# Holding each of the first 40 loads of a fused attention and gated-MLP kernel until the load four places in front of it has landed

## Chip, core and metric

The kernel runs on one core of a Trainium2 chip. The metric is the device time of one execution in microseconds (us), as a median of several runs. Engines are named as in the profile: PE (TensorE, matmuls), PEld (its weight loads), DVE (VectorE), ACT (ScalarE), POOL (GpSimd) and SP (SyncE, which here only waits and issues DMAs; its rows carry the name SPq).

## What is computed

Chunked attention, then an RMS norm and a gated MLP, all in float32:

```python
for c in range(S // 32):                       # q, k, v: (4, 8, 768, 64)
    k_ctx = k[:, :, max(0, 32*c - 16):min(S, 32*c + 40)]
    k_full = np.concatenate([mem_k, k_ctx], axis=2)      # 8 memory keys in front
    v_full = ...                                         # the same of v
    a = softmax(q_c @ k_full.T / 8)
    out[:, :, 32*c:32*c + 32] = a @ v_full
x = out.transpose(0, 2, 1, 3).reshape(3072, 512)
xn = x / sqrt(mean(x*x) + 1e-6) * rms_g
g = xn @ w_gate                                # 512 x 1536
y = (silu(g) * (xn @ w_val)) @ w_out           # w_out: 1536 x 512
```

## The kernel before

**Tiling.** Attention is cut into 32 units: batch, half of the sequence (384 tokens), pair of heads. A unit u needs three loads from DRAM, all laid out beforehand so that each is one plain transfer to 128 partitions: q (192 KB), k (312 KB) and v (384 KB). Four units with the same batch and half make one block of 384 tokens for the MLP, so there are eight blocks. The MLP's weights are cut into twelve slices of 128 hidden columns, loaded in eight groups of one or two slices for each of the three matrices (512 KB or 1,024 KB a load). Each weight and each activation is split into a high and a low part, and a product is made of three matmul passes.

**Stages.** The first stage does the attention of blocks 0 and 1 (units 0 to 7), loads and splits the weights between it, and runs the MLP of these blocks as soon as weights are there. It follows a list written out by hand, ORDER: a token is a step, with `U`n for the loads of q and k of unit n (`load_qk`), `V`n for its v (`load_v`), `Z` for the next load of weights (`w_load`), `S`n for its scores (tile s, L204), `M`, `a`, `E`, `d`, `n` for the softmax, `P`n for the transposes (pT, L283), `O`n for the product with v (o, L300), `B` and `D` for the split of the result, `G` for the sums of squares (ss, L635), `J`, `F`, `f`, `I`, `H`, `L` for turning a load of weights into its high and low part, and `g`, `v`, `o` for the MLP's products (pg, pv, po). In this stage every engine keeps the written order. Afterwards come blocks 2 and 3 with the remaining units' attention spread between their products, and then blocks 4 to 7, whose weights come back from DRAM in prepared parts.

**The queue.** Every load of q, k, v and weights is issued by SP with `nc.sync.dma_start`, in the order of the list. SP is one queue: an issue that waits holds up all issues behind it. In this text the loads are numbered by their place on SP, from 1: q0, k0, q1, k1, q2, k2, the first gate weights, q3, k3, q4, k4, q5, k5, v0, the first value weights, v1 (16), q6, k6, v2, the first output weights (20), v3, v5, v4, q7, k7, v7 (26), the second gate group (27, the first of 1,024 KB), the second value group (28), v6 (29), and from 30 to 40 weights alone.

**Waits that stand there already.** A landing is told by one of eight semaphores (DMAHW0 to DMAHW7), used in turn. A load may only be issued when the load that used its semaphore before has landed, which is the one eight places in front; so at most eight loads are under way. One tiny load from the ACT queue (rms_g) has the first use of DMAHW0. Besides, a load waits until its buffer is free: six buffers each for q, k and v (`u % 6`), and three staging buffers for weights.

Of the kernel before, what the change touches and what calls it, by code (L numbers as in the profile page):

```python
# [69 lines left out]
SEQ = ([(0, f) for f in range(FA)] + [(1, f) for f in range(FA)] + [(b, f) for f in range(FA, FC) for b in range(2)]  # L70
       + [(1, f) for f in range(FC, FF // P)])


ORDER = """
U0 U1 U2 Z U3 S0 U4 M0 a0 U5 S1 M1 a1 V0 S2 E1 E0 M2 d0 J Z V1 U6 S3 a2 n0 E2 M3 P0 V2 F S4 Z C0a a3 m0a n1 E3
# [15 lines left out]
def tile_kernel(ctx: ExitStack, tc: tile.TileContext, q, k, v, w_gate, w_val, w_out, rms_g, out):  # L91
    nc = tc.nc
# [52 lines left out]
    def late_buffers(i):  # L145
# [5 lines left out]
        else:  # L151
# [2 lines left out]
            t = p1.tile([P, KN + VN + HT], F32, name="kv0", tag="ws")  # L154
            late["kv", 0], late["pt", 1] = t[:, 0:KN + VN], t[:, KN + VN:]

    def load_qk(u):
        d = st.setdefault(u, {})
        if u < NE:
            d["q"] = early.tile([P, HT], F32, name=f"q{u}", tag=f"q{u % 6}")  # L160
            t = early.tile([P, KN], F32, name=f"k{u}", tag=f"k{u % 6}")
            nc.sync.dma_start(out=d["q"], in_=q[u])
        else:

            t = late["kv", u % 2][:, 0:KN]
            d["q"] = late["q", u % 2]
            nc.sync.dma_start(out=d["q"], in_=q[u])
        d["k"] = t.rearrange("p (j k) -> p j k", j=NJ)
        nc.sync.dma_start(out=t, in_=k[u])

    def load_v(u):
        t = early.tile([P, VN], F32, name=f"vw{u}", tag=f"v{u % 6}") if u < NE else late["kv", u % 2][:, KN:]
        st.setdefault(u, {})["v"] = t.rearrange("p (j h d) -> p j h d", j=NJ, h=2)
        nc.sync.dma_start(out=t, in_=v[u])

    def pt_of(u):

# [204 lines left out]
    def w_load():  # L382
        c = wpos["load"]
        if c >= len(wchunks):
            return
        wpos["load"] += 1
        w, k = wchunks[c]
        f, n = WGROUPS[k]
        d = wst[c] = {}
        j = c - wfirst[1]  # L390
        if j < 0:
            pool = stage if c % 3 else p1
            tag = str(c % 3) if c % 3 else ""
            s = pool.tile([P, 2, DM, 2], U32, name=f"ws{c}", tag="ws" + tag)[:, 0:n]
        elif j % 3 == 2:
            s = p1.tile([P, 1, DM, 2], U32, name=f"ws{c}", tag="wy")
        else:
            if j % 3 == 0:
                wst["pair"] = p1.tile([P, 2, DM, 2], U32, name=f"ws{c}", tag="ws")
            s = wst["pair"][:, j % 3:j % 3 + 1]  # L400
        d.update(n=n, low=s[:, :, :, 0], high=s[:, :, :, 1], top=s.bitcast(F16)[:, :, :, 1])
        nc.sync.dma_start(out=s.rearrange("p n f t -> p n (f t)"),
                          in_={"g": w_gate, "v": w_val, "o": w_out}[w][f:f + n].bitcast(U32).rearrange("n p f -> p n f"))

    def w_open(c):
# [100 lines left out]
    def moe_t(g, vv, blk):  # L506
        g = silu_r(g, blk)
        t = silu_a(g)
        silu_b(t, g)
        moe_m(t, vv)  # L510
        return t
# [51 lines left out]
    def late_steps():  # L563
# [3 lines left out]
        for n in range(len(pairs) + 1):  # L567
# [27 lines left out]
            for u in new:  # L595
                load_qk(u)
# [15 lines left out]
            for u in cur if n else ():  # L612
                load_v(u)
# [4 lines left out]
    def tok_R(n):  # L618
        late_buffers(0)
        load_qk(NE)  # L620
        load_v(NE)
# [74 lines left out]
    def tok_o(n):  # L696
# [5 lines left out]
    steps = dict(  # L702

        U=load_qk, V=load_v, Z=lambda n: w_load(), W=warm, R=tok_R,

        S=stage_s, M=stage_ma, a=stage_mb, E=stage_e, d=lambda k: stage_da(2 * k), n=stage_db,
# [511 lines left out]
    for blk, fs in segments:  # L1218
# [10 lines left out]
        for n, f in enumerate(fs):  # L1229
# [28 lines left out]
            elif blk < 3:  # L1258
                with tc.high_priority():
                    t = moe_t(g, vv, blk)  # L1260
                xs = split_x(late_x["x"], t, out_, lambda h: moe_out(fs[-1], h, po, **edge))
            else:
                with tc.high_priority():
                    t = moe_t(g, vv, blk)
# [91 lines left out]
```

## Time and profile before

| what | us |
|---|---|
| median of 3 runs | 668.07 |
| lowest and highest of them | 666.81, 669.07 |
| the profiled execution | 671.41 |
| its span, first to last instruction | 669.6 |

The rows further down come from the profiled execution alone. In a timeline a row gives the start, the duration, the engine, the line, the operation and the tiles (written <- read), with a count when alike instructions follow each other; in square brackets stands the idle time in front of it and what ended it. A row of a DMA issue gives the tiles, the count, the size in KB and the time from the start of the issue to the landing; so start plus that time is the moment of landing. A row of the view by stretches gives the stretch, its length, the busy time of the five engines with their counts, then the granted share of PE's clock (1.00 is 2.4 GHz, 0.50 is 1.2 GHz), the share of time in which the DMA engines were busy, and GB/s. That last share can pass 1 a little, since packets on one engine overlap.

### The profile page before, as it was taken

The numbers are of one execution on the slowest core, as the hardware profiler recorded it, in microseconds if no ns is written. First come the engines' busy times: TensorE is split into PE (matmuls) and PEld (weight loads), VectorE is DVE, ScalarE is ACT, GpSimd is POOL, SyncE is SP. The second block draws the span as 40 slices with busy tenths as digits, with TensorE's granted clock in tenths as the row PEclk, the third lists the DMA queues.
The fourth block names the chain that finished last, engine by engine and source line by source line (L and its number), as shares of the span: only waits on it lengthen the run. The fifth ranks groups of instructions, "written<-read, shape, count | busy, mean of one in ns | idle before, by whom it ended". The sixth has DMA issues, their size and how long they took to land.

```text
span 669.6 us, 15527 instructions
## 1 busy us (share of the span) xinstructions
PE 657.9 (98%) x6238; PEld 612.1 (91%) x6238; DVE 503.3 (75%) x1020; ACT 334.7 (50%) x642; POOL 4.7 (1%) x12
## 2 busy tenths in 40 slices
PE   6999999999999999999999999999999999999998
PEld 4898999999899999989999999999888899999997
DVE  6699999777688788877859567569638378888964
ACT  4779887843434435354445454345335233434553
POOL 0010000000000000000000000000000000000000
PEclk8699999999999999999999999999999999999999
DMA  9645454249698778345439779797643599987102
GB/s 324 251 159 181 185 189 146 106 135 351 187 374 302 254 247 291 107 168 165 143 126 369 262 235 308 253 294 256 191 142 116 170 352 331 320 303 265 52 9 71
DMA packets 82039, 145.46 MB, mean 217 GB/s; under 512 B 7472, under 2 KB 34608, under 8 KB 81968
## 3 DMA queue, kind: packets, MB, share of 16 engines
q1 hardware_dynamic: 80096, 141.32, 62.2%
q10 hardware_dynamic: 1872, 3.15, 1.4%
q8 instruction: 49, 0.80, 0.5%
q14 instruction: 22, 0.18, 0.1%
HBM read 109.84 MB, written 34.60 MB: 216 GB/s over the span
## 4 chain that ended last, share of the span: by engine, by line
PE 88%; DVE 4%; DMA 3%; ACT 2%; issue 1%; SPq 0%; DVEq 0%
PE pg L473 14%; PE po L523 14%; PE pv L473 13%; PE po L1195 8%; PE mva L949 7%; PE mga L949 7%; PE pa L1115 4%; PE mve L949 3%; PE mge L949 3%; PE pe L1115 2%; PE s L220 2%; PE oe L314 2%; PE mgc L949 2%; PE mvc L949 2%; PE pT L283 1%; DMA kv<-qp 1%
## 5 line engine op out<-in xcount | busy, mean ns | idle before, releaser
L473 PE MATMUL pg<-xh,wh_g 128*128 128x384 f32 x192 | 67.3, 351 | 0.7 <-DVE rg L482 0.7
L473 PE MATMUL pg<-xh,wl_g 128*128 128x384 f32 x192 | 65.3, 340 | 0.0
L473 PE MATMUL pg<-xl,wh_g 128*128 128x384 f32 x192 | 65.2, 340 | 0.0
L473 PE MATMUL pv<-xh,wh_v 128*128 128x384 f32 x192 | 65.2, 339 | 0.0
L473 PE MATMUL pv<-xl,wh_v 128*128 128x384 f32 x192 | 64.9, 338 | 0.0
L473 PE MATMUL pv<-xh,wl_v 128*128 128x384 f32 x192 | 64.8, 338 | 0.0
L949 PE MATMUL mva<-x,r 128*128 128x384 f32 x288 | 58.2, 337 | 0.1
L949 PE MATMUL mga<-x,r 128*128 128x384 f32 x288 | 58.2, 337 | 0.1
L523 PE MATMUL po<-wh_o,hh 128*128 128x512 f32 x141 | 56.7, 402 | 0.0
L523 PE MATMUL po<-wl_o,hh 128*128 128x512 f32 x141 | 55.7, 395 | 0.0
L523 PE MATMUL po<-wh_o,hl 128*128 128x512 f32 x141 | 55.7, 395 | 0.0
L949 PEld LDWEIGHTS mga<-x,r 128*128 128x128 f32 x288 | 50.5, 188 | 0.8 <-ACT spare L921 0.4
L949 PEld LDWEIGHTS mva<-x,r 128*128 128x128 f32 x288 | 50.6, 188 | 0.5 <-DVE h L932 0.4
L182 ACT CAST hh<-t 128x384 fp32r<-128x384 f32 x45 | 23.2, 515 | 49.4 <-PE po L523 32.9
L1195 PE MATMUL po<-r,hhs 128*128 128x512 f32 x144 | 45.5, 397 | 0.0
L473 PEld LDWEIGHTS pg<-xh,wh_g 128*128 128x128 f32 x192 | 36.4, 189 | 3.3 <-DVE rg L482 1.0
L473 PEld LDWEIGHTS pg<-xl,wh_g 128*128 128x128 f32 x192 | 36.5, 190 | 1.3
L473 PEld LDWEIGHTS pv<-xh,wh_v 128*128 128x128 f32 x192 | 36.0, 188 | 0.4
L473 PEld LDWEIGHTS pg<-xh,wl_g 128*128 128x128 f32 x192 | 36.3, 189 | 0.0
L473 PEld LDWEIGHTS pv<-xl,wh_v 128*128 128x128 f32 x192 | 36.1, 188 | 0.3
L473 PEld LDWEIGHTS pv<-xh,wl_v 128*128 128x128 f32 x192 | 36.0, 188 | 0.0
L494 DVE TENSOR_TENSOR t<-t,pv 128x384 f32<-128x384 f32 x48 | 26.4, 550 | 10.7 <-PE pv L473 9.5
(252 smaller groups left out, 1600.2 us busy)
## 6 DMA issues: line engine op xcount, KB each, us to landing
r<-kg SPq DMA_DIRECT2D x84, 256.0 KB, 4.9
r<-kv SPq DMA_DIRECT2D x84, 256.0 KB, 4.4
r<-ko SPq DMA_DIRECT2D x68, 256.0 KB, 3.9
kv<-in_v_dram SPq DMA_DIRECT2D x24, 384.0 KB, 4.8
kv<-in_k_dram SPq DMA_DIRECT2D x24, 312.0 KB, 4.1
ws<-in_moe_w_gate_dram SPq DMA_DIRECT2D x4, 1024.0 KB, 4.8
ws<-in_moe_w_val_dram SPq DMA_DIRECT2D x4, 1024.0 KB, 4.8
ws<-in_moe_w_out_dram SPq DMA_DIRECT2D x4, 1024.0 KB, 4.9
```

Of the source, the lines that this page charges most:

```text
L182: return nc.scalar.copy(out, in_)
L220: on_pe(nc.tensor.matmul(d["s"][a:a + CH, o:o + KC], lhsT=d["q"][r, c * CH:c * CH + CH], rhs=d["k"][r, c // 2, 40 * cp:40 * cp + KC], star ...
L283: on_pe(nc.tensor.transpose(out=t[:, i * P:(i + 1) * P], in_=pe[:, i * P:(i + 1) * P], identity=ident))
L314: on_pe(nc.tensor.matmul(o2[cp][64 * hh:64 * hh + 64, o:o + CH], lhsT=st[u]["v"][r, j, hh], rhs=pt[r, j, hh ^ u % 2], start=True, stop=True))
L473: on_pe(nc.tensor.matmul(ps[:, 0:HT], lhsT=weight(a, n, f, kt), rhs=xs[c][:, kt], start=kt == 0 and i == 0, stop=kt == NKT - 1 and i == 2))
L494: nc.vector.tensor_tensor(out=t, in0=t, in1=vv, op=ALU.mult)
L523: on_pe(nc.tensor.matmul(po[i], lhsT=h[a][:, i * P:(i + 1) * P], rhs=weight(c, "o", f), start=f == first and n == 0, stop=f == end and n = ...
L949: on_pe(nc.tensor.matmul(bank[w, b], lhsT=r[:, a, kt], rhs=x[:, c, kt], start=bool(first) and kt == 0 and i == 0, stop=kt == 1 and i == 2, ...
L1115: on_pe(nc.tensor.matmul(bank[c][i], lhsT=uhl[u][x][:, i * P:(i + 1) * P], rhs=w[y], start=p == 0 and n == 0 and m in (1, 2, 5), stop=p == ...
L1195: on_pe(nc.tensor.matmul(po[i], lhsT=cur[a][:, i * P:(i + 1) * P], rhs=r[c], start=f == n == 0, stop=f == NF - 1 and n == 2))
```

## The change

A new helper `held` issues the load and keeps a list of what it has sent. From the fifth load on, and up to the fortieth, it adds a dependency on the load four places in front; this is a wait on that load's semaphore in front of the issue. `load_qk`, `load_v` and `w_load` call it in place of `nc.sync.dma_start`.

```diff
+HELD = 4
+    sent = []
+
+    def held(**kw):
+        i = nc.sync.dma_start(**kw)
+        i = getattr(i, "ins", i)
+        if HELD <= len(sent) < 40:
+            tc.add_manual_dep(i, sent[-HELD].name, mybir.DependencyInfo(mybir.DependencyClass.Sync, mybir.DependencyReason.DATA),
+                              reason="few loads in flight")
+        sent.append(i)
...
-            nc.sync.dma_start(out=d["q"], in_=q[u])
+            held(out=d["q"], in_=q[u])
...
-        nc.sync.dma_start(out=t, in_=k[u])
+        held(out=t, in_=k[u])
...
-        nc.sync.dma_start(out=t, in_=v[u])
+        held(out=t, in_=v[u])
...
-        nc.sync.dma_start(out=s.rearrange("p n f t -> p n (f t)"),
+        held(out=s.rearrange("p n f t -> p n (f t)"),
```

On PE, DVE, ACT, POOL and SP the instructions stand in the same order in both kernels, and SP has 448 of them in both. What differs is what SP's issues wait for. First SP's loads 5 to 13 (q2 to k5), before:

```order
L162 DMA q2_144<-in_q_dram 128x384
L169 DMA k2_145<-in_k_dram 128x624
L402 DMA ws0_148<-in_moe_w_gate_dram 128x1024
L162 DMA q3_150<-in_q_dram 128x384 [waits DMAHW0_49]
L169 DMA k3_151<-in_k_dram 128x624 [waits DMAHW1_49]
L162 DMA q4_179<-in_q_dram 128x384 [waits DMAHW2_49]
L169 DMA k4_180<-in_k_dram 128x624 [waits DMAHW3_49]
L162 DMA q5_187<-in_q_dram 128x384 [waits DMAHW4_49]
L169 DMA k5_188<-in_k_dram 128x624 [waits DMAHW5_49]
```

The same place on SP now (L161 is the line of the helper):

```order
L161 DMA q2_144<-in_q_dram 128x384 [waits DMAHW1_49]
L161 DMA k2_145<-in_k_dram 128x624 [waits DMAHW2_49]
L161 DMA ws0_148<-in_moe_w_gate_dram 128x1024 [waits DMAHW3_49]
L161 DMA q3_150<-in_q_dram 128x384 [waits DMAHW4_49,DMAHW0_49]
L161 DMA k3_151<-in_k_dram 128x624 [waits DMAHW5_49]
L161 DMA q4_179<-in_q_dram 128x384 [waits DMAHW6_49]
L161 DMA k4_180<-in_k_dram 128x624 [waits DMAHW7_49]
L161 DMA q5_187<-in_q_dram 128x384 [waits DMAHW0_49]
L161 DMA k5_188<-in_k_dram 128x624 [waits DMAHW1_49]
```

The semaphore in a wait moved by four: k3 (load 9) waited for that of k0 (load 2, DMAHW1) and now waits for that of k2 (load 6, DMAHW5). The wait on the load eight in front is contained in it, since that one landed still earlier. The loads with the largest transfers, SP's 26 to 29, before:

```order
L174 DMA vw7_428<-in_v_dram 128x768 [waits DMAHW2_49,PE_49]
L402 DMA ws3_463<-in_moe_w_gate_dram 128x2x1024 [waits DMAHW3_49,DVE_49,Activation_49]
L402 DMA ws4_598<-in_moe_w_val_dram 128x2x1024 [waits DMAHW4_49,DVE_49,Activation_49]
L174 DMA vw6_605<-in_v_dram 128x768 [waits DMAHW5_49]
```

And the same four rows of SP now:

```order
L161 DMA vw7_428<-in_v_dram 128x768 [waits DMAHW6_49,PE_49]
L161 DMA ws3_463<-in_moe_w_gate_dram 128x2x1024 [waits DMAHW7_49,DVE_49,Activation_49]
L161 DMA ws4_598<-in_moe_w_val_dram 128x2x1024 [waits DMAHW0_49,DVE_49,Activation_49]
L161 DMA vw6_605<-in_v_dram 128x768 [waits DMAHW1_49]
```

The waits for free buffers (on PE, DVE and ACT, here Activation) stand as they were; the wait on a landing again moved by four places.

## Rows read from the trace of the kernel before

**Rows 1.** The page: busy time of each engine, share of the span.

```profile
PE 657.9 (98%) x6238; PEld 612.1 (91%) x6238; DVE 503.3 (75%) x1020; ACT 334.7 (50%) x642; POOL 4.7 (1%) x12
```

**Rows 2.** Timeline of PE, 0 to 45 us.

```profile
5.07 0.90 PE L204 MATMUL s<-k,q 64*32 64x64 f32 x48
6.55 0.90 PE L204 MATMUL s<-k,q 64*32 64x64 f32 x48 [0.59 <-DMA k<-in_k_dram]
8.56 0.90 PE L204 MATMUL s<-k,q 64*32 64x64 f32 x48 [1.11 <-DMA k<-in_k_dram]
11.17 1.28 PE L204 MATMUL s<-k,q 64*32 64x64 f32 x48 [1.71 <-DVE r L270]
...
13.39 1.52 PE L204 MATMUL s<-k,q 64*32 64x64 f32 x48
...
17.61 0.92 PE L300 MATMUL o<-pt,vw 128*64 128x64 f32 x24 [0.52 <-DMA vw<-in_v_dram]
```

**Rows 3.** Chain of waits, the piece in front of that last row.

```profile
10.26 7.22 DMA vw<-in_v_dram
```

**Rows 4.** Waits of PE from 20 us to the end: the longest.

```profile
PE pg L473 <- DVE rg L482: 0.7, 1, 0.7
```

**Rows 5.** Timeline of SP's issues, 0 to 70 us.

```profile
2.57 0.43 SPq L162 DMA_DIRECT2D q<-in_q_dram  x1
...
8.44 0.33 SPq L174 DMA_DIRECT2D vw<-in_v_dram  x1
9.75 0.33 SPq L402 DMA_DIRECT2D ws<-in_moe_w_val_dram  x1
10.26 1.49 SPq L174 DMA_DIRECT2D vw<-in_v_dram  x1
...
12.90 0.33 SPq L174 DMA_DIRECT2D vw<-in_v_dram  x1
13.40 0.33 SPq L402 DMA_DIRECT2D ws<-in_moe_w_out_dram  x1
...
17.54 0.33 SPq L162 DMA_DIRECT2D q<-in_q_dram  x1
...
19.79 0.38 SPq L402 DMA_DIRECT2D ws<-in_moe_w_gate_dram  x1
31.91 0.38 SPq L402 DMA_DIRECT2D ws<-in_moe_w_val_dram  x1
```

**Rows 6.** Loads 1, 2, 4 and 9, issued at 0.72, 1.16, 2.10, 4.47 us.

```profile
q<-in_q_dram SPq DMA_DIRECT2D x1, 192.0 KB, 2.4
k<-in_k_dram SPq DMA_DIRECT2D x1, 312.0 KB, 3.2
k<-in_k_dram SPq DMA_DIRECT2D x1, 312.0 KB, 4.3
k<-in_k_dram SPq DMA_DIRECT2D x1, 312.0 KB, 6.6
```

**Rows 7.** Loads issued on an empty queue, at 105.94 and 140.50 us.

```profile
ws<-in_moe_w_val_dram SPq DMA_DIRECT2D x1, 512.0 KB, 3.1
kv<-in_k_dram SPq DMA_DIRECT2D x1, 312.0 KB, 2.8
```

**Rows 8.** The page's DMA issues: gate loads of two slices, median to landing.

```profile
ws<-in_moe_w_gate_dram SPq DMA_DIRECT2D x4, 1024.0 KB, 4.8
```

**Rows 9.** Timeline of ACT, 38 to 40 us: first use of load 27.

```profile
38.34 1.16 ACT L417 ACTIVATE ws<-ws 128x1024 int32<-128x1024 uint32 x1
```

**Rows 10.** Busy time, clock and DMA by stretches: opening, then full queue.

```profile
1.70:6.90 5.20, 4.52 (x77) 1.86 (x81) 1.70 (x6) 0.95 (x2) 0.23 (x1) 1.00 0.96 292
6.90:26.20 19.30, 14.88 (x400) 12.69 (x391) 16.64 (x38) 12.37 (x26) 0.00 (x0) 0.80 1.03 399
```

**Rows 11.** The same view: the two stretches at PE's lower clock.

```profile
11.50:14.90 3.40, 3.25 (x92) 2.54 (x81) 3.36 (x8) 1.88 (x4) 0.00 (x0) 0.50 1.04 406
...
21.80:35.40 13.60, 13.60 (x154) 12.43 (x153) 8.00 (x19) 8.16 (x17) 1.64 (x2) 0.50 0.58 210
```

More of the change, by code (lines that the diff above doesn't have):

```diff
@@ L166, in load_qk @@
             d["q"] = late["q", u % 2]
-            nc.sync.dma_start(out=d["q"], in_=q[u])
+            held(out=d["q"], in_=q[u])
         d["k"] = t.rearrange("p (j k) -> p j k", j=NJ)
-        nc.sync.dma_start(out=t, in_=k[u])
+        held(out=t, in_=k[u])
     def load_v(u):
```

## Prediction, written before the changed kernel was run

> **What bounds the kernel now.** I read the busy times first: PE is busy 98% of the span [rows 1]. A change to loads can then only act where PE waits for one. The waits of PE are the second view: after 20 us the longest is 0.7 us, and it is for DVE [rows 4]; the first 20 us are the only place where landings set the pace. There PE's timeline is the third view [rows 2]. The scores of units 1 and 2 start after 0.59 and 1.11 us of waiting for k1 and k2. Those of unit 3 start at 11.17 us after 1.71 us that the row puts down to DVE; but k3 (load 9) was issued at 4.47 us and took 6.6 us [rows 6], so it landed at 11.1 us, and the row's releaser hides a fourth wait for a load. The product of unit 1 with v1 (load 16) waits 0.52 us and starts at 17.61 us. The chain of waits runs through that same transfer: issued at 10.26 us, 7.22 us under way, landed at 17.48 us [rows 3]. So until 17.5 us the stream of loads is the bound, and behind it PE is.
>
> The fourth view is SP's timeline [rows 5], and it has to be read as a clock of landings. From load 9 on an issue waits for the landing eight places in front, and these issues had nothing else to wait for; so the issue of load 14 at 8.44 us tells that load 6 has just landed, 9.75 us is the landing of load 7, 10.26 of load 8, 12.90 of load 11, 13.40 of load 12 and 17.54 of load 16. The last view is the stretches [rows 10]: between 6.9 and 26.2 us the DMA engines are busy without a break at 399 GB/s. A load there is under way for 6.6 or 7.2 us, and nearly all of this is standing in line.
>
> **The change, part by part.** *The issues.* 36 loads get a wait, loads 5 to 40. It binds where load n would have been issued before load n-4 landed. Load 5 was issued at 2.57 us [rows 5], and load 1, issued at 0.72 us, took 2.4 us [rows 6]: it is held until 3.1 us. So it goes on through load 27, issued at 19.79 us. Load 28 goes out at 31.91 us [rows 5], when its own buffer comes free; by then the stream has long run empty, and from there on the landing four places in front is always the older event. So 23 issues move later, and 13 added waits find their semaphore already raised. Moving an issue costs nothing by itself: what is queued on SP behind it is the next load, which is held by the same rule, and SP has no other work in this stretch. The instructions on SP are 448 in both kernels.
>
> *The landings.* What counts is whether a held load still lands when it did. It lands at the later of two moments: when the transfers in front of it are done and its own is done behind them, as before; and when its whole round trip has passed, counted from the landing of load n-4, which now releases it. On an empty queue the round trip is 2.4 us for q and 3.2 us for k at the start [rows 6], later 2.8 us for k and 3.1 us for a weight load of 512 KB [rows 7]; for v, which lies between these in size, I estimate 3.0 us from the two. Against these stands the time between two landings four places apart in the trace of before. From load 7 to load 11 it is 12.90 - 9.75 = 3.15 us, from 8 to 12 it is 13.40 - 10.26 = 3.14, from 12 to 16 it is 17.48 - 13.40 = 4.08, and from 4 to 8, with load 4 issued at 2.10 us and landed 4.3 us later [rows 6], it is 10.26 - 6.4 = 3.9. Load 8 is a q (2.4 against 3.9), load 12 a q (2.4 against 3.14), load 16 a v (3.0 against 4.08): on this path to v1 the round trip is over 0.7 to 1.5 us before the line in front has been worked off. With three loads still in line the queue does not run dry, and the landings stay where they are.
>
> The tight place is k4 and k5, loads 11 and 13. Load 11 has 3.15 us for a round trip of 2.8 to 3.2. By the rate alone four loads q, k, q, k are 1,008 KB, or 1.03 MB, at 399 GB/s: 2.6 us, and in an execution where the engines reach that, a k arrives up to 3.2 - 2.6 = 0.6 us later than it could. I bound the two at 0 and 0.6 us late and take 0 to 0.1, since 3.15 is what this place showed. The cover: the scores that use k4 start at 13.39 us [rows 2], 0.5 us after its landing at 12.90, and they stand behind transposes on PE; only the last 0.1 us of the bound would be seen. If that cover were gone, the whole 0.6 us would be on the path.
>
> *The large load.* Load 27 (1,024 KB) is now issued when load 23 has landed and not load 19, some 4 us later than 19.79 us (four places of about 1 us, which is what a v of 384 KB takes at 399 GB/s). On an empty queue it needs 4.8 us [rows 8], so even from 24 us it lands before 30; ACT first reads it at 38.34 us [rows 9]. Cost nothing, with 8 us of cover.
>
> *The sum.* 0 us for the issues, 0 for the path to v1 (between 0 and 0.1), 0 for load 27: the span stays at 669.6 us and the profiled execution at 671.41 us, 3.3 us above the median of the three runs. As a median I forecast 668.07, rounded to **668.1 us**.
>
> A bound below nothing: could fewer loads under way be better? In the opening the stream makes only 292 GB/s [rows 10], and load 4, with three in front of it, took 4.3 us. If loads 5 to 8 are what slows loads 1 to 4, holding them back lets the first four (1.03 MB) come at 399 GB/s. That is 2.6 us; started 1 us after the first issue at 0.72 us and with 0.4 us for the report at the end (the 2.4 us of load 1 are its 0.5 us at that rate and 1.9 more; I split these by estimate), load 4 lands at 4.7 us instead of 6.4. The gain ends at 1.7 us.
>
> The Trainium skill, in DMA: Bandwidth & Descriptors, "Rules for kernel authors", says to issue a transfer early and to wait for it late, so that its fixed cost is hidden, which speaks against this change; the same page ("Anatomy of one DMA", for another issuing path) puts the fixed part at about 2.0 us and the rest at 436 GB/s, from which I estimate 2.7 us for a k. By that figure k has 0.4 us to spare in the 3.15 us of its round, and the sum is 0 as well; the page's rule of thumb would cost something only where the line is shorter than the fixed part.
>
> **The rivals.** *The queue runs dry.* Held back, the stream goes on as it began, at the 292 GB/s of the opening, because engines that have finished early find nothing to do and start anew for each load. Loads 5 to 16 are 3,808 KB, 3.90 MB. They came in 17.48 - 6.4 = 11.1 us; at 292 GB/s they need 13.4, so v1 lands 2.3 us later. PE waits for v1 with nothing in between and everything on PE behind it keeps its order, so all of it reaches the end: **670.4 us**. It is slower by over 0.3% (2.0 us, about what a measurement of this kernel can tell from no change) once the three rounds to v1 take 4.4 us each on average (11.1 + 2.0, by three) instead of 3.7. For it speaks that loads 3 to 5, with two or three loads in front, are what made the slow opening: load 4 took 4.3 us [rows 6], and rounds of 4.3 would give +1.8 us. Against it: a part of those 4.3 us was standing in line too, and the share of busy DMA time in the opening was already 0.96.
>
> *The opening gets faster,* by up to the 1.7 us above: **666.4 us**. PE could use all of it, since it waits 0.59 + 1.11 + 1.71 + 0.52 = 3.9 us for loads [rows 2]. Against it: the loads land in the order of issue, so a later one stands behind an earlier one and not beside it, and load 5 is issued only 0.5 us behind load 4 (2.57 and 2.10 us) [rows 5, 6].
>
> *PE's clock.* It is granted 0.50 (1.2 GHz) in two stretches, of 3.4 and 13.6 us [rows 11], each behind waits of PE for loads, and 48 score matmuls take 1.52 us there and 0.90 at the higher level [rows 2]. A wait that moves by some tenths may shift such a stretch. One more like the short one costs 3.4 x (1 - 0.90 / 1.52) = 1.4 us: 669.5. Should the long one vanish, it gives back 5.5 us: **662.6**. The stretches need not fall alike in every run, and the three runs of before lie 2.3 us apart; that is noise for both kernels. The Trainium skill (TensorE: Matmul & The Clock Gate, "Part 1") says that the moment of a change varies from run to run because it is not tied to the start of the kernel; one profile cannot show that.
>
> *The change does not hold anything* would give 668.1 as well, but the order shows the waits, and load 5's comes too late to be empty.
>
> **How the numbers follow.** My forecast, landings unmoved, has 0.70; the dry queue 0.14; the faster opening 0.08; the clock 0.08, half on each side. Faster by over 0.3% (under 666.1): the clock's lower half, 0.04, and 0.02 each from the opening and from noise, 0.08. Slower by over 0.3% (over 670.1): 0.08 of the dry queue, 0.02 of the clock and 0.02 of noise, 0.12. Within: 0.80. The range goes from 666.2 to 670.4 us: it takes in the opening's end and the dry queue's price and leaves out the clock's far end.
>
> **What would show it.** In the profile of the changed kernel SP's issues of loads 9 to 27 stand 1 to 5 us later, each just behind the landing four places in front; a load is under way for 2.4 to 4.8 us instead of 6 to 9; the stream still makes about 400 GB/s between 6.9 and 26.2 us; PE starts the product with v1 at 17.6 us within 0.3. If that start is over 19 us and the GB/s fall to about 300, the dry queue is right; if PE starts the scores of unit 1 before 6 us, the opening is. A median beyond 2 us with the start at 17.6 would point to the clock, or to something after 20 us that I have not seen.

## The result, and the profile after

The change made the kernel slower. The median of six runs is 672.5 us (670.34 to 674.21) against 667.44 us for six runs of the kernel before (665.6 to 669.07): a ratio of 1.0082, with an interval of 1.0059 to 1.0105, or 5.1 us. A later comparison of the same two kernels gave 1.0118 (1.0084 to 1.0151). The forecast was 668.1, with a range up to 670.4. Two executions far outside all others, one of before (795.56 us) and one of the kernel long_before (2,237.8 us), are left out of all numbers here.

The two profiled executions do not show this difference as they stand: after has a span of 668.5 us and before one of 669.6 [rows 2, 10 and 11 come from it]. The one of before was a bad draw of its kernel (671.41 us, above each of its six timed runs), and the one of after the best of its six (670.34). So their totals cannot be subtracted; their first 25 us, where the change acts, can still be read.

SP's timeline of the kernel after, 0 to 36 us (start, duration, what was issued):

```profile
3.31 0.33 SPq L161 DMA_DIRECT2D q<-in_q_dram  x1
...
8.06 0.33 SPq L161 DMA_DIRECT2D q<-in_q_dram  x1
...
12.08 0.33 SPq L161 DMA_DIRECT2D k<-in_k_dram  x1
14.04 0.33 SPq L161 DMA_DIRECT2D vw<-in_v_dram  x1
...
28.92 0.38 SPq L161 DMA_DIRECT2D ws<-in_moe_w_gate_dram  x1
```

These are loads 5, 10, 13, 16 (v1) and 27, to be held against [rows 5]: 2.57 became 3.31, 10.26 became 14.04 and 19.79 became 28.92. The waits hold, as forecast. Now the chain of waits of after, from load 4 to the product of unit 1 (start, duration, what):

```profile
2.10 4.58 DMA k<-in_k_dram
...
6.76 4.50 DMA q<-in_q_dram
...
11.27 2.75 DMA q<-in_q_dram
...
14.04 6.74 DMA vw<-in_v_dram
20.78 0.14 issue
20.91 0.92 PE o L311 x24
```

This is the ring of four that the change made: load 4 releases 8, which releases 12, which releases 16. Its rounds take 4.6, 2.8 and 6.8 us, 14.1 in all from the landing of load 4 at 6.68 us, where I had counted 11.1 [rows 3, 6]. v1 lands at 20.78 us and not at 17.48; in two more traces of each kernel, told of below, it lands at 21.65 and 21.01 us in after and at 17.65 and 18.03 in before. PE's timeline shows what that did:

```profile
6.82 0.90 PE L215 MATMUL s<-k,q 64*32 64x64 f32 x48 [0.31 <-DMA k<-in_k_dram]
8.18 0.90 PE L215 MATMUL s<-k,q 64*32 64x64 f32 x48 [0.47 <-DMA k<-in_k_dram]
12.20 1.11 PE L215 MATMUL s<-k,q 64*32 64x64 f32 x48 [3.12 <-DMA k<-in_k_dram]
...
17.71 0.92 PE L311 MATMUL o<-pt,vw 128*64 128x64 f32 x24 [1.36 <-DMA vw<-in_v_dram]
...
20.91 0.92 PE L311 MATMUL o<-pt,vw 128*64 128x64 f32 x24 [1.46 <-DMA vw<-in_v_dram]
```

Against [rows 2] the waits of units 1 and 2 for k became shorter (0.59 to 0.31, 1.11 to 0.47), but unit 3 now waits 3.12 us, unit 0's product 1.36 us for v0, and unit 1's product starts at 20.91 instead of 17.61 us. The stretches (stretch, length, busy time of PE, PEld, DVE, ACT, POOL, clock, DMA share, GB/s), beside [rows 10]:

```profile
1.70:6.90 5.20, 4.79 (x57) 1.83 (x61) 1.19 (x5) 0.94 (x2) 0.23 (x1) 1.00 0.95 284
6.90:26.20 19.30, 12.90 (x360) 10.96 (x359) 14.91 (x33) 10.61 (x21) 0.00 (x0) 0.83 0.90 294
```

The opening is unchanged (292, now 284 GB/s). The stretch behind it fell from 399 to 294 GB/s, while the DMA engines still count as busy 0.90 of the time. What that busy time hides is in the view that cuts this stretch into forty slices, first after (busy tenths, GB/s), then before (GB/s):

```profile
DMA  8988977979878959697797999987678999889999
GB/s 231 264 314 284 298 205 285 385 302 260 246 295 291 246 166 261 224 301 266 255 308 291 359 402 380 336 322 275 202 139 271 382 414 401 325 240 337 352 312 337
```

```profile
GB/s 404 386 379 402 398 401 410 397 383 397 399 400 400 416 416 393 391 394 386 395 424 398 408 386 410 405 414 408 382 388 392 395 390 399 399 389 404 382 420 407
```

Before, the rate is flat; after, it dips again and again, down to 139 GB/s. I counted the packet records behind these rows: between 6.9 and 26.2 us 11 of 2,752 packets of before took over 0.25 us and twice their usual time; after, 105 of 2,061. Added up, what these took beyond the usual is 14% of the time of the 16 engines in after and 0.7% in before. The rest of the loss is engines that stand idle: at least 15 packets are under way for 99.5% of the stretch in before and for 49% in after, where there are sometimes only 5, but never none.

Where the loss ends is seen farther down. In the traces of both kernels, and of every other kernel without added matmuls that ran here, 618.6 to 619.7 us pass from the first product with the output weights (tile po, 50.2 us in before's profiled execution) to the end. So all of the difference is made in the first 50 us.

### The profile page after: what moved, and what is told of

It reads as the page before. It is cut to its first block, busy times and chain, and to the rows that moved or that the text cites. A ratio compares the mean times of both kernels' runs of the same rounds, so it can differ in the third digit from the quotient of the medians.

```text
span 668.5 us, 15524 instructions
## 1 busy us (share of the span) xinstructions
PE 655.2 (98%) x6238; PEld 609.3 (91%) x6238; DVE 503.7 (75%) x1020; ACT 334.9 (50%) x642; POOL 4.7 (1%) x12
## 4 chain that ended last, share of the span: by engine, by line
PE 92%; DVE 3%; DMA 3%; ACT 1%; issue 0%; SPq 0%; DVEq 0%
PE pg L484 15%; PE po L534 15%; PE pv L484 15%; PE po L1206 8%; PE mva L960 7%; PE mga L960 7%; PE pa L1126 4%; PE mve L960 3%; PE mge L960 3%; PE oe L325 2%; PE s L231 2%; PE pe L1126 2%; PE mgc L960 2%; PE mvc L960 2%; PE pT L294 2%; DMA q<-in_q_dram 1%
```

## Experiments

### How many loads, and which of them

Four variants of the helper: six places instead of four, three places, four places for loads 5 to 16 alone, and four places for loads 17 to 40 alone.

```diff
-HELD = 4
+HELD = 6                                  # held6;  HELD = 3 in held3
-        if HELD <= len(sent) < 40:
+        if HELD <= len(sent) < 16:         # first16
+        if 16 <= len(sent) < 40:           # late24
```

> Each of the first 40 loads waits for the landing six places in front instead of four. Dry-engines theory (one of the 16 DMA engines that is ahead runs out of work before the next load is released, starts anew, and the last of the 16 sets each landing): with five loads still in line there is nearly always work, the product with v1 starts at 17.6 to 18.5 us, 667.4 to 668.8 us. Cost-per-wait theory (the added waits on SP cost by themselves): the same number of waits, so about 672 us as with four. Clock theory (the loss is a longer stretch of PE at 1.2 GHz): any value between 667 and 672, not tied to the start of the product with v1.

> The same with three places. Dry-engines theory: loads 5 to 16 come in four rounds of about 4 us each, v1 lands at 22.5 to 24 us and the time is 675 to 678 us; the rate between 6.9 and 26.2 us falls under the 294 GB/s of four places, to 220 to 260. Cost-per-wait theory: 672 to 673 us. Clock theory: no ordered change, 670 to 674 us.

> Held four places as in the change, but only loads 5 to 16, up to v1. Theory that all of the loss arises until v1 has landed, and that later landings are early enough anyway: as the whole change, 671.5 to 673 us. Theory that loads 17 to 27, which land 2 to 5 us later in the changed kernel, delay work after 20 us as well: 669.5 to 671 us.

> Held four places, but only loads 17 to 40. Theory that all of the loss arises until v1 has landed: 667 to 668.3 us, product with v1 at 17.6 us. Theory that the later landings matter too: 669 to 670.5 us.

| kernel | median us | ratio to before | v1 lands | GB/s, 6.9 to 26.2 us |
|---|---|---|---|---|
| before (eight places) | 666.44 | 1 | 17.48 | 399 |
| held6 | 666.1 | 0.9989 (0.9971 to 1.0006) | 18.64 | 359 |
| after (four places) | see above | 1.0082 | 20.78 | 294 |
| held3 | 677.17 | 1.0153 (1.0123 to 1.0182) | 23.92 | 227 |
| first16 | 671.26 | 1.0070 (1.0037 to 1.0103) | 21.05 | 324 |
| late24 | 667.38 | 1.0007 (0.9988 to 1.0026) | 17.63 | 340 |

The rates are from the same view by stretches, here held6, held3, first16 and late24:

```profile
6.90:26.20 19.30, 14.29 (x414) 12.09 (x403) 16.71 (x38) 13.32 (x28) 0.00 (x0) 0.91 1.00 359
```

```profile
6.90:26.20 19.30, 10.82 (x295) 9.08 (x289) 12.02 (x27) 7.44 (x16) 0.00 (x0) 0.67 0.73 227
```

```profile
6.90:26.20 19.30, 13.03 (x384) 11.10 (x384) 15.00 (x33) 11.24 (x23) 0.00 (x0) 0.82 0.94 324
```

```profile
6.90:26.20 19.30, 15.44 (x425) 13.53 (x425) 17.47 (x39) 13.93 (x29) 0.00 (x0) 0.91 0.95 340
```

The rate falls step by step with the number of loads that may be under way, so it is the dry queue. It is not the added waits as such: held6 adds 34 of them and held3 37. The waits on loads 5 to 16 alone bring most of the loss (671.26 us lies between the two ranges that I had expected, and its interval takes in both); those on loads 17 to 40 lower the rate as well (340), but nothing is lost by them. A lower rate costs only where a landing is waited for. One miss: held6 lands v1 1.2 us late and was still level with before, where I had expected a small loss. Its trace shows most of the cover: behind the product with v1 the kernel before has one more stop of PE, of 0.93 us, which the view puts down to ACT, and held6 only 0.18 us at the same place. The first sums of squares thus start at 19.87 us in held6 and at 19.46 in before, only 0.4 us later. The line of before:

```profile
19.46 0.83 PE L635 MATMUL ss<-onef,xq 128*128 128x1 f32 x6 [0.93 <-ACT xh L655]
```

What this stop is comes out with the fillers below.

In the profiled executions held6 has one stretch at the lower clock in the first 60 us (3.4 us), and before two (17.0 us) [rows 11]. That led to the next question.

### Two more traces of the same kernels

> The kernel before, unchanged, for a second trace. Its first profiled execution (671.41 us) lies above its median by 3 to 4 us and had 17 us of PE's lower clock in the first 36 us. Theory that this was an untypically long low stretch: 665 to 668 us with 3 to 11 us at the lower clock and v1 landing at 17.5 to 18 us. Theory that the profile itself costs that: again about 671 us.

> The changed kernel, unchanged, for a second trace; its first one (670.34 us) was the lowest of its six times. Theory that the loss is the late landing of v1 and a longer low stretch of PE's clock together: 671.5 to 674 us, v1 landing at 20 to 22 us, 10 to 18 us at the lower clock. Theory of landings alone: the same v1, with no more time at the lower clock than in the kernel before.

Both kernels unchanged, one profiled execution each. Before took 668.55 us here (a little above its range), after 672.78. The time until the first output product, by the view by stretches (length, busy PE, and on to clock, DMA share and GB/s; three of before, then three of after; the third of each is from a comparison told of below):

```profile
0.00:50.19 50.19, 43.33 (x712) 37.30 (x713) 36.36 (x78) 31.73 (x59) 4.68 (x12) 0.83 0.68 245
```

```profile
0.00:47.53 47.53, 40.09 (x712) 34.11 (x713) 36.11 (x78) 31.58 (x59) 4.68 (x12) 0.93 0.71 258
```

```profile
0.00:47.99 47.99, 39.22 (x713) 33.53 (x713) 36.24 (x78) 31.56 (x59) 4.69 (x12) 0.93 0.71 256
```

```profile
0.00:49.39 49.39, 40.88 (x713) 34.72 (x713) 36.53 (x78) 31.88 (x59) 4.68 (x12) 0.90 0.75 249
```

```profile
0.00:51.89 51.89, 40.99 (x713) 34.81 (x713) 36.47 (x78) 32.05 (x59) 4.68 (x12) 0.87 0.73 237
```

```profile
0.00:53.13 53.13, 43.30 (x712) 37.17 (x713) 36.28 (x78) 31.72 (x59) 4.68 (x12) 0.84 0.69 232
```

Length less busy PE is PE's idle time: 6.9, 7.4 and 8.8 us in before, 8.5, 10.9 and 9.8 in after; on average 7.7 and 9.7, 2 us more. (v1 lands 3.4 us later on average; before's stop of 0.93 us ahead of the sums of squares, 1.19 and 1.26 us in its other traces, does not show in after, whose PE comes to that place later.) The busy time is that of the same matmuls and varies with the clock beside it: 43.3 us at 0.83, 40.1 at 0.93. So the loss has two parts, waits and clock, and the first execution of before that I had read from had the second part without the first. It and the third of after had the same 17.0 us at the lower clock and the same busy time; their first output products lie 2.9 us apart, which is the waits alone. All three traces of before are above the median of its executions (668.55 and 669.38 us in the new ones, against some 666.4), so they show too little of the clock's part.

### The clock: fillers in PE's waits

If the clock falls because PE waits, small matmuls on zeros in these waits should hold it up, without touching the loads. They use the kernel's own `warm` step, put into ORDER where PE waits, as `W`n for n matmuls of 64 columns. Every result stays as it was.

```diff
 # fill_before: the kernel before; fill_before_s has W5, W10, W2, W4
-... V0 S2 ... U6 S3 ... U7 O1 ... E4 G0 ...
+... V0 W20 S2 ... U6 W30 S3 ... U7 W8 O1 ... E4 W16 G0 ...
 # fill_after: the kernel after; fill_after_s has W2, W18, W8, W8
-... V0 S2 ... U6 S3 ... V5 O0 ... U7 O1 ...
+... V0 W8 S2 ... U6 W60 S3 ... V5 W24 O0 ... U7 W24 O1 ...
```

> The kernel before with 74 small matmuls (64 x 64, of zeros, into a tile that nobody reads) on PE in front of the four places where it waits in the first 20 us (20, 30, 8 and 16 of them), about 3 us in all. Theory that PE's waits lead to the lower clock: less time at 1.2 GHz than the kernel before, and 1 to 3 us faster where that had a long low stretch, 664 to 666.5 us. Theory that the clock does not follow these waits: 666.5 to 668 us, the fillers costing up to 1 us where they outlast a wait.

> The changed kernel with 116 such matmuls in front of its four waits (8, 60, 24, 24). The landings stay late. Theory of landings and clock together: the part that the clock has, 2 to 3 us, comes back, 668.5 to 670.5 us, with v1 landing at 20 to 22 us as in the changed kernel. Theory of landings alone: 671 to 673 us.

> The kernel before with such fillers of 5, 10, 2 and 4 matmuls in front of the same places (0.6, 1.3, 0.25 and 0.5 us; its waits there are 1.1, 1.7, 0.5 and 0.9). Clock theory: 0 to 3.5 us at 1.2 GHz in the first 60 us, 664.5 to 666.5 us, and the runs closer together. Landings alone: 666.4 us as the kernel before, or up to 0.5 more.

> The changed kernel again with small matmuls of zeros in front of PE's four waits, now sized by what one took (0.127 us at the higher clock): 2, 18, 8 and 8, about 0.25, 2.3, 1.0 and 1.0 us, each less than the wait there. Landings stay late (v1 at 20 to 22 us). Theory that two thirds of the loss are PE's lower clock behind longer waits: under 4 us at 1.2 GHz, 667 to 669.5 us. Theory of landings alone: 671.5 to 673.5 us, the clock changing nothing.

Measured: fill_before 673.36 us, ratio 1.0098 (1.0067 to 1.0129); fill_after 676.8, 1.0151 (1.0088 to 1.0215); fill_before_s 669.77, 1.0049 (1.0022 to 1.0075); fill_after_s 671.78, 1.0087 (1.0068 to 1.0107). The clock rose in three of the four (not in fill_before_s): in fill_after the profiled execution has no stretch at the lower level, and its mean over the runs is 0.9992 where that of after is 0.988. The times did not follow: three lie above both of their ranges, and fill_after_s where landings alone had it. The fillers cost as much as they saved, or more. In fill_before they ran past the waits (20 of them took 2.54 us). The fewer ones of fill_before_s brought a stop of another kind, in PE's timeline:

```profile
13.38 0.58 PE L204 MATMUL s<-k,q 64*32 64x64 f32 x6 [1.66 <-issue]
...
19.95 0.38 PE L204 MATMUL s<-k,q 64*32 64x64 f32 x6 [1.36 <-issue]
```

"issue" is time in which PE waited for no engine and no load. In the kernel before no such stop stands at the first of these places [rows 2]. The packet records tell what it is: the loading of PE's own program. On the queue that the profile calls instruction a piece of 16,384 bytes comes in from time to time. Counted with its weight loads, PE stops in fill_before_s at its 450th, 706th and 962nd instruction, 256 apart, and each time goes on 1.3 to 1.5 us after such a piece has landed. In long_before (below) a stop of 1.76 us and in fill_before one of 2.94 us stand at the 706th too, before other operations. At the 706th also stand before's stop of 0.93 us ahead of the sums of squares (1.56 us after the piece) and held6's of 0.18 us (1.25 us after it). Added matmuls move other work onto these places, and a PE that comes there later does not stop.

To have fewer instructions for the same fill, the filler was made eight times as long (512 columns), and one or two were used at a place. The kernel after ran unchanged beside it:

```diff
-            nc.tensor.matmul(w[0:64, 0:64], lhsT=zero, rhs=zero, start=True, stop=True)
+            nc.tensor.matmul(w[0:64], lhsT=zero, rhs=zero.unsqueeze(1).broadcast_to([P, 8, 64]), start=True, stop=True)
 # long_before: W1 ahead of S3 and G0; long_after: W2 ahead of S3, W1 ahead of O0 and of O1
```

> The kernel before with two such matmuls, in front of unit 3's scores and of the first sums of squares. Clock theory: at most 3.4 us at 1.2 GHz, 664.5 to 666 us, the upper runs gone. Idle time alone: 666.5 us.

> The changed kernel with four long matmuls of zeros (64 x 512, an estimated 0.85 us each) in front of three of PE's waits: two in front of unit 3's scores, one each in front of the products with v0 and v1. Four instructions in place of 36, so that PE's code grows by next to nothing. Theory that the waits on late loads bring the lower clock and that it makes up a third to a half of the loss: 0 to 4 us at 1.2 GHz, 669 to 671 us. Theory that the idle time alone is the loss: as the changed kernel beside it, within 0.7 us.

> The changed kernel unchanged, timed beside the next two, and a third trace. Theory of idle time and clock together: 671 to 673 us; until the first output product of blocks 0 and 1 PE idles 8 to 11 us (before: 6.6 and 7.2) and is busy for 40 to 42 us, which is 38.5 at a short low stretch of its clock and 44 at a long one.

> The kernel before, a third trace: 665 to 668 us, v1 landing at 17.4 to 17.8 us, PE idle for 6.5 to 7.2 us until the first output product, and 3 to 7 us at 1.2 GHz. If it has 17 us at 1.2 GHz again, the changed kernel's low stretches are nothing that the change brings.

Measured: long_before 667.2 us, 1.0015 (0.9996 to 1.0033), mean clock 0.998; long_after 674.4, 1.0107 (1.0065 to 1.0148), clock 0.994; after unchanged 674.83, 1.0118 (1.0084 to 1.0151), clock 0.985; one execution of before 669.38. So long_after's clock is again up and its time where it was, which is what idle time alone would give; long_before lies above both of its forecasts. after3 and before3 lie above theirs too (before3 with v1 at 18.03 us and 8.8 us idle, but with 6.8 us at the lower clock and not 17). Against the trace of after beside it, PE's idle time until the first output product fell in long_after by 2.5 us. Its busy time fell by 1.6, although the fillers themselves took 4.1. By this design the clock's price cannot be read from the times: a filler shows that waits lower the clock, and its own cost hides what that is worth.

### The clock's price, from runs of one kernel

What the fillers left open, the runs themselves tell, since executions of the same kernel differ in clock. The mean granted clock c gives the time at the lower level, 2 x (1 - c) x span, because the two levels are 1 and 0.5. Over 69 executions of before in the later comparisons (mean c 0.9956, so 5.8 us of low clock on average, 4.0 in the median one; median time 666.4 us) the span rises by 0.36 us for each us at the lower clock. My price in the forecast was 1 - 0.90 / 1.52 = 0.41.

The 11 executions of after have a mean c of 0.988, so 16.2 us at the lower clock, and a median of 673.3 us. The difference of 6.9 us then splits in this way:

- 10.4 us more at the lower clock, by 0.36: 3.7 us.
- At the same clock, 0.992: 672.3 us for after (3 executions) against 668.7 for before (7): 3.6 us. This is near the 3.3 us by which v1 lands later in the first pair of traces, and above the 2 us more of idle time in PE.

The two add up to 7.3, against 6.9 measured; that is as good as a slope over scattered runs can be. By itself it is a correlation: in a given kernel the executions with longer waits may be those with the lower clock, and the 3 executions at 0.992 are few. PE's busy time until the first output product has no waits in it, and says the same: in the twelve traces without added matmuls it is 37.9 to 38.4 us with 3.4 us at the lower clock (merged, held6, late24), 39.0 to 40.1 with 6.8 (first16, before3, merged4, before2), 43.3 with 17.0 (before, the third of after) and 44.0 with 20.5 (held3), with the other two of after in between: 0.35 us for each us. So the price is measured, as is that the clock of after is lower and its path to v1 3 us longer; that about half of the loss is clock is an estimate from these.

### Bytes or loads in line

If what counts is bytes in line, four larger loads should do. So q and k of units 0 to 7 were laid side by side in DRAM and loaded as one transfer of 504 KB, once with the kernel's own eight semaphores, and once held by four places.

```diff
-            nc.sync.dma_start(out=d["q"], in_=q[u])
-            nc.sync.dma_start(out=t, in_=k[u])
+            nc.sync.dma_start(out=qk, in_=q[u])      # q and k side by side; held(...) in merged4, for 32 loads
```

> The kernel before with q and k of units 0 to 7 side by side in DRAM and in one load of 504 KB each; so the same bytes in 8 fewer loads, not held. It is the base for the next one. No theory of the holding speaks of it: 665.5 to 667.5 us, v1 (now load 10) at 17 to 18 us.

> The same merged loads, each held for the landing four places in front, up to the same load of weights as in the change. Dry-engines theory (what counts is how many bytes still stand in line when a load is released): three loads of 384 to 512 KB are about 1.4 MB, as much as five of the smaller ones, so like holding six places: v1 at 17.5 to 19 us and 0 to 1.5 us over the merged one. Theory that four places are too few whatever the size, since each held load pays a restart: v1 at 20 us or later and 3 to 6 us over the merged one.

| kernel | median us | ratio to before | v1 lands |
|---|---|---|---|
| merged | 665.36 (10 runs, 664.66 to 665.69) | 0.9980 (0.9967 to 0.9993) | 16.50 |
| merged4 | 665.89 | 0.9995 (0.9984 to 1.0006) | 16.48 |

The stretch behind the opening, merged first, then merged4:

```profile
6.90:26.20 19.30, 14.92 (x422) 13.10 (x412) 17.48 (x39) 14.07 (x29) 0.00 (x0) 0.91 1.00 397
```

```profile
6.90:26.20 19.30, 14.99 (x416) 13.16 (x405) 17.42 (x40) 14.06 (x29) 0.00 (x0) 0.91 0.96 347
```

Both land v1 earlier than expected. merged4 has the same rule of four places as the changed kernel and loses nothing on the way to v1: 16.48 us. So the number of places is not what costs. In the changed kernel a load up to v1 has three in front of it, 0.9 MB on average, and the rate was 294 GB/s; five of them (held6, 1.5 MB) gave 359, and three of merged4 (1.5 MB as well) 347, enough not to be late. Bytes in line are not the whole rule: between 6.9 and 16.5 us held6 makes 326 GB/s and merged4 386 with the same bytes in front, so the size of a load counts as well; which of the two counts for how much was not separated. merged is the fastest kernel of this study, below before by 0.2%, with v1 landing 1 us earlier at the same 397 GB/s; it has 8 loads fewer, and its opening (1.7 to 6.9 us) makes 349 GB/s, as merged4's does (348), where before's makes 292.

## Why the prediction was wrong

*What bounds the kernel.* Right in the place: everything is decided before the first output product, on the path to v1, and nothing behind it changed (618.6 to 619.7 us from there to the end). Wrong in one reading: I noted that the profiled execution lay 3.3 us above the median and went on. It had 17.0 us at the lower clock [rows 11], where this kernel has 5.8 on average; that clock is worth as much (11.2 x 0.36 = 4.0, by the slope above).

*The issues.* Right in the main: the added waits moved loads 5 to 27 (load 27 by 9.1 us, where I had expected up to 5), and no time was lost on SP. Loads 28 and 29 went out 1.8 us later too; SP waited there for DVE, which set the staging buffer free later.

*The landings.* This is the step that failed: "With three loads still in line the queue does not run dry, and the landings stay where they are." I compared the round trip of one load on an empty queue (2.4 to 3.2 us) with the time between landings four places apart (3.14 to 4.08) and found room. Both rows were right, and they do not answer the question. Of a held load in the middle of this stream three single issues of after show (queue, size, us to landing), at 10.29, 12.08 and 14.04 us:

```profile
k<-in_k_dram SPq DMA_DIRECT2D x1, 312.0 KB, 3.2
...
k<-in_k_dram SPq DMA_DIRECT2D x1, 312.0 KB, 4.6
...
vw<-in_v_dram SPq DMA_DIRECT2D x1, 384.0 KB, 6.7
```

The lone k took 2.8 us [rows 7]; the held ones of this stream up to 4.9 (k3, issued at 7.20 us), for a held load has others in front of it and those run at 294 GB/s, not at 399. Each load has sixteen updates of its semaphore in the trace, taken here as one from each of the 16 engines, and its landing is the last of them. For v1 they are spread over 2.0 us in before and 2.2 in after, for a load on an empty queue (30 to 32 of before) over 0.25 to 0.53. So one of the 16 engines can be through with its part of the loads in line about 2 us before the last, and then has nothing to do until the next issue. A start after idling is slow: in the four places of before where a load meets an empty queue, between 48 and 66 us, its first packet starts 1.0 us behind the issue, and 13 to 16 of its 256 packets, all but one among the first sixteen, took 0.25 to 1.08 us where the median is 0.16. With three loads in line some engines can be at that point while others are still behind, so the line as a whole is never dry and yet the rate falls by a quarter. One such load in before (1,024 KB, on an empty queue, 60 to 64.4 us) shows the restart by itself:

```profile
DMA  0000009993001289998999999999999999910000
GB/s 0 0 0 0 0 0 149 223 112 37 0 0 37 112 335 372 410 559 335 447 410 410 410 410 447 410 484 410 410 372 410 447 410 447 484 38 0 0 0 0
```

This part rests on counted packets, on the spread of the updates and on the order of the rates. The records do not name a packet's engine, and no run here took the restart away by itself.

The rival *The queue runs dry* had this: its rate of 292 GB/s (measured 294), its sign in the profile ("if that start is over 19 us": 20.91) and most of its size (v1 2.3 us later; measured 3.3 us). Its 670.4 us fell short, for it had no term for the clock; and it let all of v1's delay reach the end, where the stop behind the product with v1 covers about 1 us. That its rate came out so near is in part luck: by 4 us eight loads were issued in before, so the opening is no sample of a line of four, and the other two traces of after make 269 and 286 GB/s in that stretch. I gave it 0.14 because the opening's DMA share of 0.96 seemed to say that the engines had no gaps. After shows 0.90 at 294 GB/s: the share counts a slow packet as busy and is no measure of how well the line is filled.

*PE's clock.* Taken as noise on both sides, and that is the second step that failed. Its price was about right (0.41 against 0.36 us for each us), its sign was not free: the waits that the change adds are what lets the clock fall. After's two stretches of the lower clock, in the same view as [rows 11]:

```profile
12.70:16.10 3.40, 3.40 (x82) 2.65 (x70) 2.72 (x7) 1.47 (x3) 0.00 (x0) 0.50 0.92 251
```

```profile
23.00:29.80 6.80, 6.80 (x107) 6.18 (x108) 4.74 (x11) 4.35 (x10) 0.00 (x0) 0.50 0.93 328
```

The first begins 0.5 us behind the end of the wait of 3.12 us, the second 2 us behind that of 1.46 us; PE is busy throughout both. (The last wait ahead of before's long stretch was not for a load, as I had it, but the stop of 0.93 us for instructions.) The Trainium skill (TensorE: Matmul & The Clock Gate, Part 1) tells of the same thing for a matmul whose waits for loads let the clock go down again and again; the clocks of 0.988 and 0.9956 on average agree with that. By the estimate above, the added waits of PE in this stretch cost about twice their length.

*The large load.* I had it land before 30 us. It was issued at 28.92 us and landed at 35.7, since its place in the ring is released by load 23 and the whole stream is late. The cover held: ACT reads it at 37.55 us, where it did at 38.34 [rows 9].

```profile
37.55 1.15 ACT L428 ACTIVATE ws<-ws 128x1024 int32<-128x1024 uint32 x1
```

Of the 8 us of cover 2 are left, and the answer "cost nothing" was right with a term that was 6 us off.

*The opening gets faster.* A little of it is there: units 1 and 2 wait 0.28 and 0.64 us less. But load 4 landed at 6.68 us, not earlier than in before (6.4), so holding back the loads behind it did not speed it up.

## What to carry to other kernels

What keeps a queue of loads at its rate is how much is in line, not the fact that something is: here 0.9 MB in front of each load gave 294 GB/s and 1.5 MB about 350, so when the number of loads under way is cut, make the loads larger first (one transfer for q and k was worth 0.2% by itself). Do not price a held stream by a lone load on an idle queue. Before a profiled execution is used as the base of a sum, compare its time and its clock with the other runs; and where the trace shows the clock falling behind waits, give the clock a term of its own beside the wait.

## What the runs showed of the hardware that was not expected

- The lower clock lasts through stretches in which PE is busy without a gap: 6.80 of 6.80 us in after, 13.60 of 13.60 in before [rows 11].
- The DMA share of a stretch can stay at 0.90 while the rate falls from 399 to 294 GB/s.
- PE stops for its own program: at its 450th, 706th and 962nd instruction, 1.66, 1.36 and 0.56 us in fill_before_s, until 1.3 to 1.5 us after a piece of 16,384 bytes has landed. In before 0.93 us of this stand on the path and are put down to ACT by the view.
- The sixteen updates of one load were spread over 2.0 us (v1 in before) and 2.2 us (v1 in after) in the stream, and over 0.25 to 0.53 us on an empty queue.
